# The copies of N to the substitution's tile: the order in which ScalarE walks them (RWKV-7 attention and a gated MLP, one core)

## The chip, the cores and the metric

The kernel runs on one core of one Trainium2 chip. The metric is the device time of one execution in microseconds (us); lower is better. The times are medians over several runs.

## The reference, cut to what matters

The first block is a recurrent attention (4 batches, 8 heads, 768 steps, head dimension 40). Each step reads from a 40x40 state per head and then updates it:

```python
y[:, :, t] = einsum('bhd,bhde->bhe', rt, state)
Sa = einsum('bhde,bhe->bhd', state, at)
state = state * wt[:, :, None, :] - einsum('bhd,bhe->bhde', Sa, bt) \
        + einsum('bhd,bhe->bhde', vt, kt)
```

Its output, as 3072 tokens of 320 numbers, goes through `h = x @ w_in` (320x2048), `g = h * cos(h)` and `g @ w_out` (2048x320). All of it is in float32; the two weights arrive in double precision and are rounded in the kernel.

## The kernel before, in words

The 768 steps are cut into chunks of 64 (C), and a "unit" u is one chunk of two batches with all eight heads, so there are 24 units. Within a chunk the step-by-step update becomes a triangular system: a matrix N of products of b and a between the steps of the chunk has to be inverted. The kernel inverts blocks of 32 (Q = 32) by a back substitution on VectorE, four units at a time, and joins the two blocks of a chunk with small matmuls (the tiles called `beside`).

N is made in `p1_n(u)`, for two units at a time. TensorE fills a PSUM tile `nps` whose word order is unit (written c), head (j) and step (t), with t innermost; the two halves of the heads (e) stand in two PSUM banks. From there ScalarE (called ACT in the profile) makes two kinds of copies:

- The diagonal blocks go to the SBUF tile `nt`, whose word order within a partition is step t, unit, e, j. Along t its step is 32 words. For the units 0 to 3 (L447) there are two copies of 128 partitions by 256 words for each call; for all later units (L455) there are four of 32 partitions by 512 words. With 24 units that is 4 copies of the first form and ten groups of four of the second.
- `lower()` (the segment `lo` of the plan, L466 and L474) later copies the other blocks to `noff` and `rt`. Both sides of these copies are walked in runs of 32 words or more.

Once four units stand in `nt`, `inv_start` (L493) turns it with one transpose of VectorE into `u`, and `inverse` runs 31 steps of two VectorE instructions (L501, L505), two transposes at the end (L518, L509) among them. The result is read by `beside_first` and `beside_second`, and by `ch_s`.

The order of work is written out by hand. A string, `PLAN`, lists segments (`pn4`, `lo4`, `k2`, `T1`, `M` for a piece of the MLP, `r` for one step of its cosine, `i` for a step of the inverse), and each engine takes its instructions in that order, with no reordering at run time. The PSUM tiles called `at` (`nps` except for unit 2, and the transposes, `gram`, `x0ps`, `sps`, `dps`, `qps`) share a pool of two buffers, so a later one of them waits until the copies out of the one before the last have been made. In the MLP, `ph` is the first product, `turns` its cosine argument (ACT L853, L860 and L861, VectorE L857), `gT` the product (VectorE L864) and `po` the second matmul.

The function that the diff touches, and what calls it:

Of the kernel before, what the change touches and what calls it, by code (L numbers as in the profile page):

```python
# [20 lines left out]
def kernel(  # L21
# [15 lines left out]
    Q = C // 2  # L37
    HB = Q // 2
    NB = P // C
    HH = H // 2  # L40
# [7 lines left out]
    quad = [slice(Q * i, Q * i + Q) for i in range(4)]  # L48
# [25 lines left out]
    def mm(o, lhsT, rhs, start, stop=True):  # L74
        nc.tensor.matmul(o, lhsT=lhsT, rhs=rhs, start=start, stop=stop, skip_group_check=True)  # L75

    def pick(t, offset, *dims):

        return bass.AP(t.tensor, t.offset + offset, [list(t.ap[0]), *(list(d) for d in dims)])
# [6 lines left out]
    G = {"rest": [], "outs": []}  # L86
# [15 lines left out]
    for n, fill in (("w", 1.0), ("a", 0.0), ("b", 0.0)):  # L102
        for i in range(4):
            x = slice((i - 2) * H * DP, (i - 1) * H * DP)
            if i < 2:
                t = const.tile([P, H, DP], F32, tag=f"nat_{n}{i}", name=f"nat_{n}{i}")
            else:
                t = {
                    "w": w_in_sb[:, 0, late:], "a": w_in_sb[:, 1, late:], "b": late_out
                }[n][:, x].rearrange("p (h d) -> p h d", h=H)  # L110
# [211 lines left out]
    def at(name):  # L322
        return ps_a.tile([P, 2, 512], F32, tag="at", name=name)

    def one(pool, name):
        if pool is None:
            return at(name)[:, 0]
        return pool.tile([P, 512], F32, tag="h" if pool is ps_h else "o", name=name)
# [81 lines left out]
    def p1_n(u):  # L410
        if u == 2:
            ps = [one(ps_h, "nps") for _ in range(2)]
        else:
            pair = at("nps")
            ps = [pair[:, e] for e in range(2)]


        for i in range(2):
            for j in range(4):
                o = (4 * i + j) * Q  # L420
                for bb in range(NB):
                    for e in range(2):
                        bT, aT = G["bT", u + i][half[e], j], G["aT", u + i][half[e], j]
                        if u >= 4:
                            mm(
                                pick(ps[e][blk[bb ^ e]], o, (8 * Q, 2), (1, Q)), bT[:, blk[bb]],
                                aT[:, blk[bb]], i == 0 and j == 0,
                            )
                            continue
                        for m in range(2):  # L430
                            x = slice(C * bb + Q * m, C * bb + Q * m + Q)
                            to = ps[e][quad[2 * (bb ^ e) + m]]
                            first = i == 0 and j == 0
                            if m:
                                mm(to[:, o : o + Q], bT[:, x], aT[:, x], first)
                            else:
                                mm(
                                    pick(to, o, (8 * Q, 2), (1, Q)), bT[:, x], aT[:, blk[bb]],
                                    first,
                                )  # L440

        if u % 4 == 0:
            G["nt"] = sb1.tile([P, Q, 4, 2, HH], F32, tag="nt", name="nt")
            G["rtq", u // 4] = sb2.tile([P, 4, H, C], F32, tag="rt", name="rt")
        if u < 4:
            for e in range(2):
                nc.scalar.copy(  # L447
                    G["nt"][:, :, u % 4 : u % 4 + 2, e, :].rearrange("p t c j -> p c j t"),
                    ps[e][:, : 2 * HH * Q].rearrange("p (c j t) -> p c j t", c=2, j=HH),
                )  # L450
        else:

            for n in range(4):
                o = 8 * Q * (n % 2)
                nc.scalar.copy(  # L455
                    G["nt"][quad[n], :, u % 4 : u % 4 + 2].rearrange("p t c e j -> p e c j t"),
                    pair[quad[n], :, o : o + 8 * Q].rearrange("p e (c j t) -> p e c j t", c=2, j=HH),
                )

        def lower():  # L460
            if u < 4:
                noff = late_out[:, Q * H * u : Q * H * (u + 2)].rearrange(
                    "p (c e j t) -> p c e j t", c=2, e=2, j=HH
                )
                for e in range(2):
                    nc.scalar.copy(  # L466
                        noff[:, :, e].rearrange("p c j t -> p c (j t)"),
                        ps[e][:, : 2 * HH * Q].rearrange("p (c n) -> p c n", c=2),
                    )
                G["noff", u // 2] = noff  # L470
            rt = G["rtq", u // 4]
            for g in range(NB):
                for e in range(2):
                    nc.scalar.copy(  # L474
                        rt[quad[2 * g], u % 4 : u % 4 + 2, HH * e : HH * e + HH, Q:],
                        ps[e][quad[2 * g], 8 * Q :].rearrange("p (c j t) -> p c j t", c=2, j=HH),
                    )

        G["lower", u] = lower
# [476 lines left out]
    def n_of(u):  # L956
        needs(f"pb{u}")
        p1_n(u)
# [254 lines left out]
```

## Time and profile before

| | |
|---|---|
| Median of 3 runs | 806.73 us (804.41 to 807.42) |
| The profiled execution's own time | 803.6 us |
| Its span, first to last instruction | 801.9 us |
| TensorE (PE) busy | 721.6 us, 90% of the span |
| VectorE (DVE) busy | 509.3 us, 64% |
| ScalarE (ACT) busy | 432.2 us, 54% |
| GpSimd (POOL) busy | 192.8 us, 24% |

The profiled execution is 3.1 us shorter than the median and 0.8 us shorter than the fastest of the three runs; it is one execution, and its durations are those of that one. In the first 165 us of the span PE is busy for 112 us and VectorE for 129 us; from 165 us on PE is busy for 610 of 637 us. ("x4" behind a group is the number of its instructions; "idle before" is the time in which the engine stood still just ahead of them, with what ended that.)

### The profile page before, as it was taken

How to read it: one execution, taken by the hardware profiler on the slowest of the kernel's cores; microseconds unless marked ns; L12 is line 12 of the kernel's file. 1: busy time of each engine (PE TensorE's matmuls, PEld its weight loads, DVE VectorE, ACT ScalarE, POOL GpSimd, SP SyncE). 2: the span in 40 equal slices, each digit the busy share in tenths (PEclk: the TensorE clock that was granted, in tenths of full speed). 3: DMA queues.
4: the chain of work that ended last, by engine and by line, in shares of the span. 5: the costliest groups of instructions: out<-in, count | busy, mean ns of one | idle time of the engine just before them, and what ended most of it. 6: DMA issues, size and time to landing. Idle time of an engine off the chain costs nothing.

```text
span 801.9 us, 27337 instructions
## 1 busy us (share of the span) xinstructions
PE 721.6 (90%) x11880; PEld 569.9 (71%) x11880; DVE 509.3 (64%) x969; ACT 432.2 (54%) x760; POOL 192.8 (24%) x305
## 2 busy tenths in 40 slices
PE   4538778979998998999999989999999999999995
PEld 3437666756776787778778768877878777877773
DVE  6896877799668885577873387854456673433331
ACT  0334468745586357674557555466574556353442
POOL 4233634340522243111232111232010320301000
PEclk9556799999999999999999999999999999999999
DMA  9534556442424334433421312330231111100000
GB/s 160 124 87 115 171 108 159 106 101 59 81 59 117 60 63 81 92 70 65 72 66 44 61 28 63 65 72 11 44 62 26 40 42 36 36 20 28 19 17 17
DMA packets 180536, 55.05 MB, mean 69 GB/s; under 512 B 154432, under 2 KB 176000, under 8 KB 180416
## 3 DMA queue, kind: packets, MB, share of 16 engines
q1 hardware_dynamic: 163328, 50.35, 28.4%
q10 hardware_dynamic: 16896, 2.62, 2.1%
q8 instruction: 94, 1.54, 0.8%
q0 software_dynamic: 192, 0.33, 0.3%
q14 instruction: 26, 0.21, 0.1%
HBM read 42.07 MB, written 11.14 MB: 66 GB/s over the span
## 4 chain that ended last, share of the span: by engine, by line
PE 67%; DVE 12%; ACT 10%; DMA 3%; issue 3%; SPq 2%; POOL 1%; ACTq 0%; DVEq 0%; POOLq 0%
PE po L75 22%; PE ph L75 22%; ACT nt L455 4%; PE x0ps L75 4%; PE dps L75 3%; PE gram L75 3%; PE beside L75 3%; PE vT L333 2%; PE sps L75 2%; DVE inv_tmp L501 2%; DVE inv L505 1%; PE qps L75 1%; PE nps L75 1%; DMA nat_a<-in_a_dram 1%; PE wT L333 1%
## 5 line engine op out<-in xcount | busy, mean ns | idle before, releaser
L75 PE MATMUL po<-w_out_sb,gT 128*128 128x320 f32 x768 | 225.0, 443 | 0.0
L75 PE MATMUL ph<-xT,w_in_sb 128*128 128x256 f32 x768 | 184.4, 389 | 3.6 <-DVE gT L864 3.5
L75 PEld LDWEIGHTS po<-w_out_sb,gT 128*128 128x128 f32 x768 | 142.7, 193 | 56.3 <-issue 4.6
L75 PEld LDWEIGHTS ph<-xT,w_in_sb 128*128 128x128 f32 x768 | 142.6, 192 | 30.6 <-issue 6.2
L853 ACT ACTIVATE turns<-ph,rnd 128x512 f32<-128x512 f32 x96 | 62.1, 685 | 134.0 <-PE ph L75 126.1
L857 DVE SCALAR_TENSOR_TENSOR turns<-turns,ph 128x512 f32<-128x512 f32 x96 | 63.8, 682 | 92.9 <-ACT turns L853 92.8
L864 DVE TENSOR_TENSOR gT<-ph,turns 128x512 f32<-128x512 f32 x96 | 65.3, 685 | 37.1 <-ACT turns L861 36.9
L773 POOL TENSOR_TENSOR qz<-qz,wc 128x160 f32<-128x160 f32 x44 | 21.2, 485 | 245.6 <-DVE qz L772 244.2
L861 ACT ACTIVATE turns<-turns,half_pi 128x512 f32<-128x512 f32 x96 | 69.3, 722 | 3.1
L860 ACT ACTIVATE turns<-turns 128x512 f32<-128x512 f32 x96 | 60.2, 628 | 16.7 <-DVE turns L857 13.0
L505 DVE TENSOR_TENSOR inv<-inv,inv_tmp 128x31 f32<-128x31 f32 (+15 forms) x155 | 61.4, 396 | 5.3
L501 DVE TENSOR_TENSOR inv_tmp<-u,inv 128x31 f32<-128x31 f32 (+15 forms) x155 | 60.3, 389 | 3.0
L75 PE MATMUL ph<-xT,w_in_tail 64*64 64x256 f32 (+1 forms) x704 | 52.4, 386 | 0.0
L455 ACT COPY nt<-nps 32x512 f32<-32x512 f32 x40 | 41.9, 1047 | 6.8 <-PE nps L75 6.4
L370 DVE RECIPROCAL rw<-nat_w 128x320 f32<-128x320 f32 x20 | 42.8, 2142 | 0.2 <-POOL kn L624 0.2
L788 POOL TENSOR_TENSOR yt<-yt,wb 128x512 f32<-128x512 f32 x24 | 31.4, 1310 | 38.4 <-DVE yt L783 38.4
L746 DVE TENSOR_TENSOR sm<-sps,su 128x256 f32<-128x256 f32 x48 | 18.1, 418 | 32.1 <-ACT sm L741 31.1
L75 PEld LDWEIGHTS ph<-xT,w_in_tail 64*64 64x64 f32 (+1 forms) x704 | 26.8, 138 | 15.9 <-issue 10.6
L724 DVE COPY x<-x0ps 128x416 f32<-128x416 f32 x24 | 14.1, 588 | 34.9 <-ACT x L723 34.9
L692 ACT COPY qz<-qps 40x512 f32<-40x512 f32 x44 | 25.4, 577 | 19.7 <-PE qps L75 19.3
L371 POOL TENSOR_TENSOR bn<-nat_b,rw 128x320 f32<-128x320 f32 x22 | 19.8, 901 | 65.3 <-DVE rw L370 38.0
L75 PEld LDWEIGHTS x0ps<-vvm,ag 64*64 64x64 f32 x768 | 19.6, 140 | 12.1 <-issue 7.9
(147 smaller groups left out, 1107.0 us busy)
## 6 DMA issues: line engine op xcount, KB each, us to landing
rp<-in_r_dram SPq DMA_DIRECT2D x96, 40.0 KB
vp<-in_v_dram SPq DMA_DIRECT2D x96, 40.0 KB
xd<-yt SPq DMA_DIRECT2D x48, 80.0 KB
out_dram<-ot SPq DMA_DIRECT2D x24, 160.0 KB
nat_k<-in_k_dram SPq DMA_DIRECT2D x42, 80.0 KB
ws<-in_w_dram SPq DMA_DIRECT2D x5, 640.0 KB
wd<-ws SPq DMA_DIRECT2D x5, 640.0 KB
xT<-xd SPq DMA_DIRECT2D x24, 128.0 KB
```

The source lines that it names most:

```text
L75: nc.tensor.matmul(o, lhsT=lhsT, rhs=rhs, start=start, stop=stop, skip_group_check=True)
L370: nc.vector.reciprocal(rw, wn)
L455: nc.scalar.copy(G["nt"][quad[n], :, u % 4 : u % 4 + 2].rearrange("p t c e j -> p e c j t"), pair[quad[n], :, o : o + 8 * Q].rearrange("p ...
L501: nc.vector.tensor_tensor(tmp, u[:, j : j + 1, :j].to_broadcast([P, Q - j, j]), x[:, j:, j : j + 1].to_broadcast([P, Q - j, j]), ALU.mult,)
L505: nc.vector.tensor_tensor(x[:, j:, :j], x[:, j:, :j], tmp, ALU.subtract)
L692: nc.scalar.copy(pick(z[rows], 0, (NZ - C, 2), (NZ, 2 * NB), (1, C)), ps[rows, :, : 2 * NB * C].rearrange("p f (i t) -> p f i t", t=C),)
L788: nc.gpsimd.tensor_tensor(yt.rearrange("p j b t -> p (j b) t"), yt.rearrange("p j b t -> p (j b) t"), wx, ALU.mult)
L853: nc.scalar.activation(n, u, ACTF.Identity, bias=rnd, scale=1.0)
L857: nc.vector.scalar_tensor_tensor(ns[e], ns[e], -ROUND, us[e], ALU.add, ALU.subtract)
L860: nc.scalar.activation(n, n, ACTF.Abs)
L861: nc.scalar.activation(n, n, ACTF.Sin, bias=half_pi, scale=-2.0 * math.pi)
L864: nc.vector.tensor_tensor(gT[:, 2 * e : 2 * e + 2].rearrange("p f t -> p (f t)"), us[e], ns[e], ALU.mult)
```

## The change

Both sides of each copy to `nt` are walked in another order. Before, the source is walked as it lies in PSUM (t innermost, runs of 32 neighbouring words), and the destination has a step of 32 words from one word to the next. After, the destination is walked as it lies in SBUF: runs of 4 words in the first form and of 16 words in the second, while the source has a step of 32 words from one word to the next, over j and c in one bank in the first form, and over j, e (the other bank) and c in the second. The words copied, the numbers of instructions, partitions and words in each, the engine and the plan stay as they are.

```diff
         if u < 4:
             for e in range(2):
                 nc.scalar.copy(
-                    G["nt"][:, :, u % 4 : u % 4 + 2, e, :].rearrange("p t c j -> p c j t"),
-                    ps[e][:, : 2 * HH * Q].rearrange("p (c j t) -> p c j t", c=2, j=HH),
+                    G["nt"][:, :, u % 4 : u % 4 + 2, e, :],
+                    ps[e][:, : 2 * HH * Q].rearrange("p (c j t) -> p t c j", c=2, j=HH),
                 )
         else:
 
             for n in range(4):
                 o = 8 * Q * (n % 2)
                 nc.scalar.copy(
-                    G["nt"][quad[n], :, u % 4 : u % 4 + 2].rearrange("p t c e j -> p e c j t"),
-                    pair[quad[n], :, o : o + 8 * Q].rearrange("p e (c j t) -> p e c j t", c=2, j=HH),
+                    G["nt"][quad[n], :, u % 4 : u % 4 + 2],
+                    pair[quad[n], :, o : o + 8 * Q].rearrange("p e (c j t) -> p t c e j", c=2, j=HH),
                 )
```

## The prediction

> **What bounds the kernel now.** I read the busy times first, then the chain of work that ended last. Both are on the page:
>
> ```profile
> PE 721.6 (90%) x11880; PEld 569.9 (71%) x11880; DVE 509.3 (64%) x969; ACT 432.2 (54%) x760; POOL 192.8 (24%) x305
> ...
> PE 67%; DVE 12%; ACT 10%; DMA 3%; issue 3%; SPq 2%; POOL 1%; ACTq 0%; DVEq 0%; POOLq 0%
> ```
>
> TensorE (PE) is the bound over the whole, and its 80 us of idle time are all that any other engine can give back. ScalarE (ACT) carries 10% of the chain, and the line of the chain by lines puts 4% of the span (32 us) on L455, one of the two lines changed; its 40 copies are busy for 41.9 us. So three quarters of that work lies on the chain. Next, the groups by shape on ACT. The columns are busy us and mean ns of one, then the idle time ahead:
>
> ```profile
> L455 ACT COPY nt<-nps 32x512 f32<-32x512 f32 x40 | 41.9, 1047 | 6.8 <-PE nps L75 6.4
> L474 ACT COPY rt<-nps 32x256 f32<-32x256 f32 x48 | 15.1, 360 | 0.2
> L645 ACT COPY kT<-kT 128x512 f32<-128x512 f32 x24 | 14.0, 585 | 6.0 <-PE kT L333 4.8 <-issue 1.1
> L618 ACT COPY rt<-beside 32x512 f32<-32x512 f32 x24 | 13.8, 575 | 2.5 <-PE beside L75 2.0
> L447 ACT COPY nt<-nps 128x256 f32<-128x256 f32 x4 | 2.1, 622 | 1.6 <-PE nps L75 1.6
> L466 ACT COPY w_out_sb<-nps 128x256 f32<-128x256 f32 x4 | 1.3, 376 | 1.1 <-DMA rp<-in_r_dram 1.1
> L348 ACT COPY w<-wT 128x8 f32<-128x8 f32 x4 | 0.5, 174 | 10.8 <-PE wT L333 10.8
> ```
>
> The first and fourth rows have the same engine, operation, shape and kind of tiles; only the order of the words written differs. Writing SBUF in steps of 32 words costs 1047 - 575 = 472 ns in 512 words, 0.92 ns a word. L447 against L466, both out of `nps`, says the same: 622 - 376 = 246 ns in 256 words, 0.96 ns a word. Whatever the other side costs, this is what the change takes away.
>
> **The instructions.** The copies stay 4 of 128x256 and 40 of 32x512, in the same places of ACT's order, and nothing moves on the other four engines; no wait is added. All that changes is the duration of one copy, and with it when its readers and the later work of ACT start.
>
> **The new duration.** No large copy in this trace reads PSUM in steps, so I bound it. Below: no row shows a stepped read beating a dense one, so 575 ns (L618) for the second form and 376 ns (L466) for the first are the lower end. Above: the only stepped read of PSUM on ACT is L348, 8 words 64 words apart, in 174 ns. A line through the 128-row copies (585 ns at 512 words, 376 at 256) gives 0.816 ns a word and 167 ns at none, so 174 ns at 8 words: no surcharge. A line through the 32-row copies (575 at 512, 360 at 256) gives 0.84 and 145; against that one, L348's 8 words take 29 ns, 3.6 ns each, and 512 would take 145 + 1850 = about 2000 ns. So the bounds are 575 and 2000 ns, and the copy gets slower than today's 1047 from about 1.75 ns a word. I take 575 to 620 ns, since L348 has 128 rows as the first line has. It is a weak witness: it also writes SBUF in steps, and 8 x 0.92 = 7 ns of that ought to show and doesn't, so eight words may just fit a buffer.
>
> VectorE's transposes of 128x1024 add a hint on steps in SBUF:
>
> ```profile
> L509 DVE STREAM_TRANSPOSE rt<-inv 128x1024 f32<-128x1024 f32 x6 | 11.7, 1944 | 0.0
> L518 DVE STREAM_TRANSPOSE rn<-inv 128x1024 f32<-128x1024 f32 x5 | 10.6, 2114 | 0.1
> L493 DVE STREAM_TRANSPOSE u<-nt 128x1024 f32<-128x1024 f32 x6 | 7.4, 1242 | 9.5 <-ACT nt L455 7.7 <-ACT nt L447 1.8
> ```
>
> L493 is dense on both sides, L509 writes in steps (+702 ns), L518 reads in steps as well (+170 more). There the step on the write is the dear one and that on the read the cheap one. But it is another engine and SBUF, and a read could hide under the slow write.
>
> The rule that speaks against the change is in the Trainium skill, page "PSUM — Partial Sum Buffer", section "Specifications (TRN2)": PSUM has lines of 8 bytes; the page "SBUF — State Buffer", section "Door 1: The DMA port swizzle", gives SBUF lines of 16 bytes, and says that full rate needs two accesses to a line. A step of 128 bytes has one access to a line in either memory, so by it the read would pay as the write did. The trace agrees for the write (1047 against 575 ns); for the read it has only L348. The rule comes back as the second rival.
>
> **What the path gets.** A group of four copies would end 4 x 472 = 1.89 us earlier. What that is worth is what stands still behind it, so I went through the timeline around each of the ten groups. Two of them, with the idle time of an engine and what ended it in brackets:
>
> ```profile
> 226.34 4.25 ACT L455 COPY nt<-nps 32x512 f32<-32x512 f32 x4
> ...
> 230.60 1.27 ACT L474 COPY rt<-nps 32x256 f32<-32x256 f32 x4
> ...
> 231.92 1.09 PE L333 MATMUL aps<-ident,nat_a 128*128 128x128 f32 x8 [1.14 <-ACT rt L474]
> ...
> 242.48 1.25 DVE L493 STREAM_TRANSPOSE u<-nt 128x1024 f32<-128x1024 f32 x1 [1.90 <-ACT nt L455]
> ...
> 250.01 0.94 PE L75 MATMUL x0ps<-vvm,ag 64*64 64x104 f32 x32 [1.79 <-DVE vvm L663]
> ```
>
> In the first, PE wants the buffer that `nps` holds, and gets it when the last `rt` copy has read it; PE has 1.14 us to win, then it is its own bound. In the second VectorE waits 1.90 us for `nt` and is then busy without a pause up to `vvm`, for which PE waits 1.79 us. Read so, group by group (start of the copies in us; what is won):
>
> - 128.8: `gram` waits 0.43 us for `kT`, which is behind the copies on ACT; VectorE then waits 2.39 us for a `sign` of the weights behind them, and PE 1.96 us for VectorE's `vvm`. 1.7.
> - 154.3: VectorE waits 3.22 and 0.97 us for ACT's `sign` and `turns`, and is on the chain from 161 to 184 us. The tails of `ph` end at 158.9 and hold `turns` there. 1.5.
> - 226.3: 1.14. 238.2: 1.8 (both shown).
> - 312.3: `kT` waits 1.47 us for `rt`. 1.47.
> - 342.9: `x0ps` waits 0.41 us for `s`, `qps` 0.22 us for `rt`. 0.63.
> - 426.3: PE does not stand still. 0.
> - 457.8: `kT` waits 2.15 us for VectorE's `sm`, which waits for ACT's `sm` right behind the copies. 1.85.
> - 544.7: `gram` waits 1.09 us for `kT`. 1.09.
> - 582.5: `qps` waits 1.74 us for `rt`. 1.74.
>
> That is 12.9 us. The two copies of the first form at 33.6 us have VectorE waiting 1.79 us for them; 2 x 246 ns is 0.5. Sum 13.4 us. I take 12: in the first two groups ACT, VectorE and the DMAs take turns on the chain, and one of them may be late for a reason of its own. So the profiled execution's 803.6 us would become 791.6, and since the median of the runs is 3.1 us above it, the median would become 794.7 us, 1.5% less. If everything that ACT saves arrived (ten times 1.89 and 1.0) it would be 19.9 us; if only PE's direct waits for ACT counted (0.43, 0.86 for `sT` at 162.95, 1.14, 0.42 for `vT` at 243.11, 1.47, 0.63, 1.09 and 1.74), 7.8.
>
> **Rivals.**
>
> First, slower: the stepped read costs more than the stepped write did. The place is the same ten groups, the price the duration of one copy, and it decides from 1.75 ns a word. ACT is the last to arrive behind nine of ten groups, so every microsecond more is paid in full there. Half way between 1.75 and the bound of 3.6 ns a word a copy takes 145 + 512 x 2.7 = 1530 ns, 480 ns more; nine groups of four make 17 us and the first form adds about one: 825 us. At the bound it is 36 us or so, 843. For it: the read order takes four words in one bank, then four in the other, a walk that no row of the trace has, and L348 has 8 words only. Against it: L348 on the line with the same row count, and the cheap read of L518.
>
> Second, no change: the read in steps runs at about half rate as the write did, 167 + 512 x 2 x 0.816 = 1003 ns, 44 ns less a copy, 0.18 us a group, at most 1.7 us in all: 805.5 us. This is what the skill's rule would make of it; for it speaks that the write shows just such a doubling.
>
> Third, the copies get faster but only the direct waits shrink, because VectorE's and the DMAs' own chains are as late as before: the 7.8 us above, 799 us. This is inside the forecast's side.
>
> **How the numbers follow.** Faster 0.62 (forecast 0.50 around 794.7, third rival 0.12); no change 0.12; slower 0.26. About 0.5%, 4 us, is what a measurement of this kernel can tell from no change. The forecast with the third rival spans 787 (all that ACT saves) to 800 or so. To leave out no more than 2 in 10 the range also takes in the case of no change, and the nearer part of the slower case, up to 818: a copy of about 1380 ns. The likeliest case alone is 787 to 800.
>
> **What would show it.** The rows of L455 and L447 in the profile after decide at once: 575 to 620 and 376 to 400 ns for the forecast, about 1000 for the second rival, above 1047 for the first. If they fall, ACT's busy time drops by some 20 us to 412, L455 leaves the chain, and the brackets above (`aps` behind `rt`, `u` behind `nt`, `qps` behind `rt`) shrink to nothing or name another engine. The forecast is wrong if L455 stays above 900 ns, or if it falls and those idle times of PE stay.

## The result, and the profile after

The changed kernel takes 792.3 us (median; 791.64 to 793.06), and the kernel before, run beside it, 805.57 us. The ratio is 0.9834, with a 95% interval of 0.9808 to 0.9861: 13.3 us less, where the forecast had 12. A second comparison, shown below, gave 0.9829 (0.9797 to 0.9861). The profiled execution took 791.87 us, with a span of 790.1. Two executions of the experiments below, of 944.9 and 1814.66 us where the others of their kernels took about 800, are left out of their ratios.

The busy times and the chain by engine, from the page after:

```profile
PE 715.3 (91%) x11880; PEld 566.6 (72%) x11880; DVE 512.3 (65%) x969; ACT 413.0 (52%) x760; POOL 193.7 (25%) x305
...
PE 72%; DVE 13%; ACT 5%; DMA 3%; issue 3%; SPq 1%; POOL 0%; ACTq 0%; DVEq 0%; POOLq 0%
```

ScalarE is busy for 19.2 us less, and its part of the chain is halved; L455 is gone from the chain by lines. The groups by shape on ACT (busy us and mean ns of one) say why:

```profile
L455 ACT COPY nt<-nps 32x512 f32<-32x512 f32 x40 | 23.0, 575 | 6.4 <-PE nps L75 6.0
...
L618 ACT COPY rt<-beside 32x512 f32<-32x512 f32 x24 | 13.8, 574 | 2.7 <-PE beside L75 2.4
L466 ACT COPY w_out_sb<-nps 128x256 f32<-128x256 f32 x4 | 1.3, 376 | 0.9 <-DMA rp<-in_r_dram 0.9
L447 ACT COPY nt<-nps 128x256 f32<-128x256 f32 x4 | 1.3, 370 | 1.1 <-PE nps L75 1.1
```

L455 fell from 1047 to 575 ns, the duration of the dense copy of the same shape (L618), and L447 from 622 to 370 ns, about that of L466 (376). The stepped read of PSUM costs nothing that these rows show.

The timeline after, at the two places that the prediction showed:

```profile
224.87 2.34 ACT L455 COPY nt<-nps 32x512 f32<-32x512 f32 x4
227.23 1.27 ACT L474 COPY rt<-nps 32x256 f32<-32x256 f32 x4
...
229.15 1.04 PE L333 MATMUL aps<-ident,nat_a 128*128 128x128 f32 x8
...
237.25 1.24 DVE L493 STREAM_TRANSPOSE u<-nt 128x1024 f32<-128x1024 f32 x1
237.33 2.91 POOL L173 TENSOR_TENSOR ws<-ws,we 128x1280 f32<-128x1280 f32 x1 [8.01 <-DVE ws L168]
...
238.53 1.76 DVE L501 TENSOR_TENSOR inv_tmp<-u,inv 128x31 f32<-128x31 f32 x1
...
246.46 1.21 PE L75 MATMUL x0ps<-vvm,ag 64*64 64x104 f32 x32 [2.38 <-DVE vvm L663]
```

At the first place the bracket behind `aps` (1.14 us before) is gone. At the second, the wait of VectorE for `nt` (1.90 us) is gone too, but PE's wait for `vvm` did not shrink: it grew from 1.79 to 2.38 us. VectorE starts 1.9 us earlier against PE's own work there, and now meets GpSimd's join of `ws` (L173), which had run beside VectorE's wait and its transpose before. The first step of the inverse takes 1.76 us instead of 0.69, and the second (L505, at 240.32 us) 0.80 instead of 0.36. Counted from the start of the copies, `vvm` is ready only 0.2 us earlier than before (11.43 us against 11.63), while PE arrives 0.8 us earlier (9.20 against 9.99), because its short waits for ScalarE ahead of that are gone (0.42 us for `kT` among them); so its wait grows.

What follows that wait is a second surprise. The stretches behind two waits, the one at 463 us in the kernel before and the one at 246 us in the kernel after (length, then busy us and number of instructions of PE, its weight loads, VectorE, ScalarE and GpSimd, then the granted clock, the DMA share and GB/s):

```profile
464.10:467.50 3.40, 3.40 (x8) 2.11 (x7) 2.77 (x8) 3.18 (x6) 0.00 (x0) 0.50 0.00 0
467.50:470.00 2.50, 2.50 (x11) 1.74 (x10) 1.81 (x6) 0.72 (x1) 0.00 (x0) 1.00 0.00 0
```

```profile
247.10:250.50 3.40, 3.40 (x51) 2.65 (x44) 3.23 (x8) 2.40 (x4) 0.00 (x0) 0.51 0.81 230
250.50:252.00 1.50, 1.50 (x16) 0.82 (x19) 0.90 (x3) 0.14 (x1) 0.00 (x0) 1.00 0.40 69
```

After a stop of PE of 2.15 and of 2.38 us the granted clock is halved for 3.4 us. As an estimate, a PE that is busy all that time loses half of it, about 1.7 us; the experiments below measure 1.4 to 1.8. So a wait's price was not only its own length. In these two executions the kernel before paid this at 463 us, and the kernel after no longer does; it pays at 246 us instead.

### The profile page after: what moved, and what is told of

The parts are those of the page before. It is cut to its first block, busy times and chain, and to the rows that moved or that the text cites. A ratio compares the mean times of both kernels' runs of the same rounds, so it can differ in the third digit from the quotient of the medians.

```text
span 790.1 us, 27337 instructions
## 1 busy us (share of the span) xinstructions
PE 715.3 (91%) x11880; PEld 566.6 (72%) x11880; DVE 512.3 (65%) x969; ACT 413.0 (52%) x760; POOL 193.7 (25%) x305
## 4 chain that ended last, share of the span: by engine, by line
PE 72%; DVE 13%; ACT 5%; DMA 3%; issue 3%; SPq 1%; POOL 0%; ACTq 0%; DVEq 0%; POOLq 0%
PE ph L75 25%; PE po L75 24%; PE dps L75 4%; PE x0ps L75 4%; PE gram L75 2%; PE vT L333 2%; PE beside L75 2%; DVE inv_tmp L501 2%; PE sps L75 2%; DMA nat_a<-in_a_dram 2%; DVE inv L505 1%; DVE rw L370 1%; PE qps L75 1%; PE nps L75 1%; PE aps L333 1%
## 5 line engine op out<-in xcount | busy, mean ns | idle before, releaser
L75 PE MATMUL po<-w_out_sb,gT 128*128 128x320 f32 x768 | 222.6, 439 | 0.0
L75 PE MATMUL ph<-xT,w_in_sb 128*128 128x256 f32 x768 | 185.1, 390 | 3.8 <-DVE gT L864 3.7
L75 PEld LDWEIGHTS po<-w_out_sb,gT 128*128 128x128 f32 x768 | 141.3, 191 | 55.4 <-issue 3.0
L75 PEld LDWEIGHTS ph<-xT,w_in_sb 128*128 128x128 f32 x768 | 143.1, 193 | 31.2 <-issue 6.2
L505 DVE TENSOR_TENSOR inv<-inv,inv_tmp 128x31 f32<-128x31 f32 (+15 forms) x155 | 61.3, 395 | 5.3
L501 DVE TENSOR_TENSOR inv_tmp<-u,inv 128x31 f32<-128x31 f32 (+15 forms) x155 | 62.5, 403 | 3.0
L75 PE MATMUL ph<-xT,w_in_tail 64*64 64x256 f32 (+1 forms) x704 | 52.2, 386 | 0.0
L75 PEld LDWEIGHTS ph<-xT,w_in_tail 64*64 64x64 f32 (+1 forms) x704 | 26.5, 137 | 16.0 <-issue 10.3
L724 DVE COPY x<-x0ps 128x416 f32<-128x416 f32 x24 | 14.1, 588 | 33.6 <-ACT x L723 33.6
L75 PE MATMUL dps<-vvm,kn 64*64 64x104 f32 x768 | 23.6, 263 | 4.6 <-DVE sm L746 4.1
L75 PEld LDWEIGHTS x0ps<-vvm,ag 64*64 64x64 f32 x768 | 18.6, 134 | 12.0 <-issue 8.5
```

Source lines behind the costliest of these rows:

```text
L501: nc.vector.tensor_tensor(tmp, u[:, j : j + 1, :j].to_broadcast([P, Q - j, j]), x[:, j:, j : j + 1].to_broadcast([P, Q - j, j]), ALU.mult,)
L505: nc.vector.tensor_tensor(x[:, j:, :j], x[:, j:, :j], tmp, ALU.subtract)
```

## The experiments

**Which groups pay.** Three kernels give the new order to a part of the units only, each by a condition such as this one:

```diff
+                if u in (4, 6):
+                    nc.scalar.copy(  # the new order
+                        ...
+                    )
+                    continue
                 nc.scalar.copy(  # the order of before
```

> Only the copies of the units 4 and 6 (the two earliest groups of four) take the new order; all else is as before. Theory (a group ends 1.89 us earlier, and what stands still behind it moves up): 3.2 us less than before by the prediction's 1.7 and 1.5. Rival (only the direct waits of the tensor engine for the scalar engine shrink, 0.43 and 0.86): 1.3 us less. Rival (paid in full): 3.8 us less. The copies of these groups measure 575 ns, the others 1047 ns.

> Only the copies of the units 8, 10, 12 and 14 take the new order (226, 238, 312 and 343 us in the trace of before). Theory as the prediction has it: 1.14 + 1.8 + 1.47 + 0.63 = 5.0 us less. Theory as the trace of after corrects it: the vector engine, started 1.9 us earlier at 238 us, runs into GpSimd's join of ws, the tensor engine waits 2.4 us for vvm and its granted clock then falls to 0.50, so the second group brings nothing or costs up to 1.5: about 1.14 + 0 + 1.47 + 0.63 = 3.2 us less, or 1.7. Rival (direct waits only): 3.7 us less. The granted clock right behind 248 us tells the first two apart.

> Only the copies of the units 16, 18, 20 and 22 take the new order (426, 458, 545 and 583 us before). Theory as predicted: 0 + 1.85 + 1.09 + 1.74 = 4.7 us less. Theory as the trace of after corrects it: the wait of 2.15 us at 461 us is also what lets the granted clock fall to 0.63 and 0.81 behind it before, so removing it brings some 1.7 us more: 6.4 us less. Rival (direct waits only): 2.8 us less. The granted clock from 463 to 470 us tells the first two apart: 1.00 if the correction holds.

Measured against before: the units 4 and 6 give 0.9965 (0.9942 to 0.9987), that is 2.8 us, between 1.0 and 4.7; the units 8 to 14 give 0.9973 (0.9948 to 0.9998), 2.2 us (0.2 to 4.2); the units 16 to 22 give 0.9939 (0.9914 to 0.9964), 4.9 us (2.9 to 6.9). The first and the last hold the predicted 3.2 and 4.7 us. The first also holds both its rivals (1.3 and 3.8 us); the last also holds the 6.4 us with the clock, and leaves the 2.8 us of the direct waits just outside. The middle one excludes the predicted 5.0 us, and holds the corrected 1.7 to 3.2 us and the 3.7 us of the direct waits.

The traces tell more, since a stretch can be measured from the start of one group of copies to the next. From the group at 426 us to the end, the old order took 373.8 us in each of the first two of these kernels, where the wait of 2.15 us at `kT` is there but the clock does not fall behind it, and 375.6 us in the kernel before, where it does. With the new order it takes 368.8 us in the third and 369.1 in the kernel after. So the predicted waits give 4.9 us (4.7 predicted), and the fall of the clock 1.8 us on top where it happens. From the group at 226 us to the one at 426 us the old order took 199.9, 199.4 and 199.2 us, and the new order 196.2 (after) and 196.1 (second kernel), both with the clock at half behind `vvm`: 3.4 us less, not the 5.0 of the prediction. Taken apart from group to group, those at 226, 312 and 343 us brought 1.9, 1.7 and 1.1 us, more than the 1.14, 1.47 and 0.63 listed. From the group at 238 us to the next the old order took 73.4 to 74.1 us, and the new one 75.1 and 75.2 with the clock's fall, and 73.8 in a later run of it without (the last experiment): this group brought nothing, and the fall cost about 1.4 us. The clock behind `kT` in the third kernel is 1.00 from 467 to 472 us. It is at full rate, as expected, but so it is in the two kernels with the wait. So a fall does not follow every such wait; the last experiment comes back to this.

From the first group (129 us) to the third (226 us) the old order took 97.6, 96.8 and 98.6 us, and the new order 92.2 (after) and 92.6 (first kernel). That is 5 us, more than the listed 3.2. In all three traces of the old order the clock falls at the wait for `vvm` that follows the first group, in the two of the new order it does not. Two later kernels with the new order (the five steps ahead of `g7`, and the new order again) settle what is the clock's: theirs falls twice in this stretch, as that of the kernel before does, at partly other places, and they take 94.2 and 94.6 us. That is 3.0 to 3.3 us less than the kernel before, which is the listed 3.2.

**The same copies, made twice.**

```diff
-            for n in range(4):
+            for n in (0, 0, 1, 1, 2, 2, 3, 3):
```

> The new order, but each of the 40 copies of 32x512 is made twice, one right after the other, which gives the scalar engine back the time that the new order saved: 2 x 575 = 1150 ns a pair against 1047 ns of one copy before. Theory (the gain is the scalar engine's time and nothing else): near before, about 3 us over it: 10 groups x 4 x 0.1 us less the 0.5 us of the first form, 808 to 810 us. Rival (what the slow writes cost others, by holding the SBUF or the tile, is the gain): stays near after, 792 to 796 us.

Measured: 813.48 us, ratio 1.0113 (1.0081 to 1.0145). So the gain is ScalarE's time, and the rival is out: with the new order but the time given back, nothing of the 13 us is left. That it is 9 us slower than before, and not 3, has to be explained. Eight copies take 4.78 us, 0.54 us more than the four of before, which is 5 us in nine groups. The waits behind them are longer by as much (`kT` 2.77 us, `gram` 1.68, `qps` 2.24), and the clock falls behind three of the later ones. Behind 130 us, and without the last few us, it is at half for 24 us in this trace, against 10 in that of the kernel before. Behind the group at 317 us, for instance:

```profile
322.00:326.00 4.00, 2.63 (x116) 2.56 (x120) 0.69 (x1) 3.93 (x9) 0.90 (x2) 0.82 0.59 157
326.00:330.00 4.00, 4.00 (x31) 2.70 (x24) 3.35 (x4) 0.97 (x2) 0.00 (x0) 0.50 0.17 68
```

**The steps alone.** A kernel that holds nothing but copies, four of each, with TensorE idle:

> No part of the computation: single copies of 512 words on 128 partitions, four of each, first on the scalar engine and then on the vector engine, with one side walked in steps (read PSUM by 2, 4, 32 words; write SBUF by 2, 4, 8, 32; both by 32; read SBUF by 4, 32; write PSUM by 32), copies of 8 words dense and in steps of 64 on either side, and the two forms of the 32x512 copy with the tensor engine idle; the output is not the reference's. Theory (a step on the write to SBUF is what costs, a step on the read of PSUM costs nothing): scalar engine 585 ns dense and for every PSUM step, about 1050 for an SBUF write step of 32 with or without a stepped read; 575 and 1047 ns for the kernel's two forms. Rival (any step costs, and the kernel's new form escapes because it takes turns between two banks): about 1000 ns for the PSUM step of 32 in one bank. Eight words: if the stepped write shows 7 ns more than the dense one, the 8-word row could have shown a price; if not, it could not.

The rows of ScalarE for 512 words on 128 partitions. L60 is dense on both sides; L63 reads PSUM in steps of 32 words; L64 and L65 write SBUF in steps of 2 and 4; L68 does both in steps of 32, and L73 writes PSUM so. L96 and L97 are the new and the old form of the kernel's copy, and L74, L75 and L76 copy 8 words, dense, with a stepped read and with a stepped write:

```profile
L65 ACT COPY sout<-pair 128x512 f32<-128x512 f32 x4 | 4.2, 1055 | 0.1
...
L68 ACT COPY sout<-pair 128x512 f32<-128x512 f32 x4 | 4.1, 1015 | 0.1
L97 ACT COPY sout<-pair 32x512 f32<-32x512 f32 x4 | 4.0, 1005 | 0.1
...
L64 ACT COPY sout<-pair 128x512 f32<-128x512 f32 x4 | 2.4, 608 | 0.1
L73 ACT COPY pout<-sin 128x512 f32<-128x512 f32 x4 | 2.4, 589 | 0.1
...
L63 ACT COPY sout<-pair 128x512 f32<-128x512 f32 x4 | 2.3, 586 | 0.1
...
L60 ACT COPY sout<-pair 128x512 f32<-128x512 f32 x4 | 2.3, 586 | 3.3 <-DVE sout L45 3.2
L96 ACT COPY sout<-pair 32x512 f32<-32x512 f32 x4 | 2.3, 575 | 46.8 <-DVE sout L93 46.7
...
L76 ACT COPY sout<-pair 128x8 f32<-128x8 f32 x4 | 0.7, 173 | 0.1
L75 ACT COPY sout<-pair 128x8 f32<-128x8 f32 x4 | 0.7, 166 | 0.1
L74 ACT COPY sout<-pair 128x8 f32<-128x8 f32 x4 | 0.7, 164 | 0.1
```

In PSUM a step of any length measured is all but free, on the read (586 ns for 2, 4 and 32 words) and on the write (589 for 32). It is not the change of banks that saves the new form, for L63 stays in one bank. In SBUF a step of 2 words on the write costs 22 ns in 512 words. With steps of 4, 8 and 32 words on the write the copy takes 1015 to 1073 ns, and with steps of 4 and 32 on the read 1060 to 1088, against 617 for a dense read of SBUF; a stepped read of PSUM adds nothing to that (L68). VectorE shows the same pattern: 691 to 692 ns for reads of PSUM, dense and in all steps, 1054 for an SBUF write in steps of 4, and 1014 for one of 32. And 8 words do show the price of a stepped write: 173 against 164 ns. The kernel's old form takes 1005 ns here and 1047 in the kernel; the cause of that difference is open.

**Why the group at 238 us brought nothing.** Three kernels change the plan, on top of the new order.

```diff
-pn10 i i M i o k6 i i lo10 wj3 i i i M v7 g6 M i ag6 r r r q6 i M i i i r K7 ws3 xa6 k7 ...
+pn10 i i M i o k6 i i lo10 i i i M v7 g6 M i ag6 r r r q6 i M i i i r K7 wj3 ws3 xa6 k7 ...
```

> The new order, and in the plan GpSimd's join of ws (2.9 us, at 237 us) is moved behind the kn of unit 7, nothing else. Theory (a vector instruction with two SBUF operands stands still while GpSimd works, which is why the first steps of the inverse take 1.76 and 0.80 us there against 0.20 elsewhere): the first two steps take about 0.2 to 0.9 us, vvm is ready about 1.5 us earlier, and the wait of 2.4 us at 246 us falls to about 1; 789 to 792 us. The join then stretches whatever vector work stands beside it later. Rival (those steps are long for another reason, such as u just having been written): their durations stay at 1.7 and 0.8 us.

Measured: 792.62 us, 0.9839 (0.9813 to 0.9865), the same as the new order. From its timeline:

```profile
240.34 0.19 DVE L505 TENSOR_TENSOR inv<-inv,inv_tmp 128x31 f32<-128x31 f32 x1
...
242.43 2.93 POOL L173 TENSOR_TENSOR ws<-ws,we 128x1280 f32<-128x1280 f32 x1
242.62 2.86 DVE L505 TENSOR_TENSOR inv<-inv,inv_tmp 128x112 f32<-128x112 f32 x1
```

The first steps fell to 0.19 us each, so it was GpSimd that had stretched them: the join the first, and by the timeline after its next instruction, `kn` (0.88 us), the second. But the join now stands against a later step, which takes 2.86 us instead of 0.28 and ends 0.1 us behind it. `vvm` was no earlier (0.9 us later, counted from the copies), and PE's wait was 3.29 us, not the 1 us expected: the block moved with the join. The Trainium skill, page "SBUF — State Buffer", section "Terms", says that VectorE and GpSimd share a pair of SBUF ports, held by one for a whole instruction while the other stands still; by that rule the step has to wait out the join, and the trace agrees (2.86 against 2.93 us).

The next kernel takes five of the inverse's steps out of the way of `g6`, first to places ahead of `g7`:

```diff
-pn10 i i M i o k6 i i lo10 wj3 i i i M v7 g6 M i ag6 r r r q6 i M i i i r K7 ws3 xa6 k7 Lk8 wf4 r i Lv8 M i i Lr9 i t7
+pn10 i i M i o k6 lo10 wj3 M v7 g6 M i ag6 r r r q6 i M i i i r K7 ws3 xa6 k7 i i Lk8 wf4 r i Lv8 M i i i i Lr9 i i t7
```

> The new order, and in the plan five of the inverse's steps that stand between pn10 and g6 are moved behind g6 and q6, so that the vector engine reaches ag and vvm of unit 6 earlier. Theory (the gain of the group at 238 us was lost because vvm is late: the tensor engine stands still for 2.4 us at 246 us, and the granted clock may fall to 0.50 for one stretch of 3.4 us behind it): that wait falls under 1 us, the clock stays at 1.00 there, and the time falls by 1.5 to 4 us from the new order's, to 788 to 791 us. Rival (the steps are only late somewhere else, and the wait reappears behind the later turns): within 1 us of the new order.

Measured: 795.01 us, 0.9869 (0.9841 to 0.9898), no better than the new order (2.4 us over the kernel with the later join, which ran beside it). The wait at 246 us is gone, but the rival was right about the wait, if not about "within 1 us":

```profile
260.54 1.67 PE L75 MATMUL dps<-vvm,kn 64*64 64x104 f32 x32 [4.52 <-DVE vvm L663]
```

The moved steps stand ahead of the next unit's `vvm` now, and the clock is at half for 6.8 us at this wait. The last pair puts them behind `g7`, one by one, and runs the new order again beside it:

```diff
-pn10 i i M i o k6 i i lo10 wj3 i i i M v7 g6 ... T6 M i r K8 ag7 ... q7 r M i i M r X6 i i r
+pn10 i i M i o k6 lo10 wj3 M v7 g6 ... T6 i M i i r K8 ag7 ... q7 r i M i i i M r X6 i i i r
```

> The new order, and five steps of the inverse are moved from between pn10 and g6 to places behind g7. Theory (in the first attempt the moved steps stood ahead of g7 and made its vvm late by 4.5 us at 260 us): both waits for vvm, at 246 and at 260 us, are under 1 us, the granted clock stays at 1.00 from 240 to 300 us, and the time is 1.5 to 4 us under the new order's: 788 to 791 us. Rival (the vector engine is the bound in this stretch, so the steps are late wherever they are put): a wait of over 2 us for some vector result later on, and no less than 792 us.

> The new order itself, once more, for the comparison on this chip. 790 to 794 us as before. Theory (the granted clock halves for stretches of 3.4 us after some stops of the tensor engine of about 2 us, not after all): the same wait of about 2.4 us for vvm at 246 us, with or without a fall of the clock behind it.

Measured: 788.18 us, 0.9777 (0.9752 to 0.9802), against 792.89 us, 0.9829 (0.9797 to 0.9861), for the new order again. The two intervals overlap only at their edges, so this version beats both kernels, by 4.7 us over the new order in the medians. The traces show 1.5 us of that, against this second trace of the new order, and 2.4 against the first, in the stretch with the moved steps (193.8 us from the third group to the seventh, against 195.2 and 196.2); where the rest comes from is not shown. Neither `x0ps` at 242.6 us nor `dps` at 254.2 has a wait in its trace, and the clock holds (busy time by engine, then the clock, as above):

```profile
243.00:248.00 5.00, 5.00 (x102) 3.79 (x95) 3.07 (x9) 4.27 (x9) 0.00 (x0) 1.00 0.67 173
248.00:258.00 10.00, 9.90 (x194) 8.19 (x193) 9.16 (x23) 3.53 (x9) 0.54 (x2) 1.00 0.22 36
```

In the new order's second trace the wait for `vvm` is 2.36 us at 251.8 us, all but the 2.38 of the first; behind it the clock stays up:

```profile
252.50:255.90 3.40, 3.40 (x69) 2.40 (x64) 3.23 (x8) 2.69 (x5) 0.00 (x0) 1.00 0.87 240
```

The ten traces of the whole kernel show what tells the two apart. In each of them every change of the granted clock lies on a grid of its own, with steps of 3.41 us. Here is the step of that grid that holds the wait in the trace after, and the two over which the same wait is spread in the second trace of the new order:

```profile
243.59:247.00 3.41, 1.03 (x27) 0.66 (x29) 3.24 (x10) 0.69 (x1) 0.00 (x0) 1.00 0.49 83
```

```profile
246.82:250.23 3.41, 2.64 (x24) 1.64 (x16) 3.03 (x12) 1.37 (x2) 0.01 (x1) 1.00 0.82 247
250.23:253.64 3.41, 1.81 (x66) 1.68 (x67) 3.38 (x8) 0.64 (x2) 0.00 (x0) 1.00 0.32 68
```

PE is busy for 0.30 of the step in the first, and for 0.77 and 0.53 in the second. Over all ten traces, except their last few us, the clock fell after each of the 22 steps at full clock in which PE was busy for less than 0.44 of the time, after 42 of the 85 between 0.44 and 0.63, and after none of the 1905 above. By these counts a stop of about 2 us costs more when it falls into one step than when a border cuts it; between 0.44 and 0.63 PE's busy time alone does not decide.

## Why the prediction was right, and where it was not

- **The price of the write.** Right: the copies gave back 472 and 252 ns of the forecast 472 and 246.
- **The price of the read.** The lower bound (575 ns) was the truth, and the rivals that hang on this price, slower and no change, are out. The hint from L509 and L518 was no evidence for it. On VectorE a stepped read of SBUF is indeed the cheaper one (596 ns against 427 dense, where a stepped write takes 1014 against 692), but on ScalarE it costs as much as a stepped write (1060 against 617 dense), and neither says anything of PSUM. The reasoning about L348 was wrong in one point: eight words do pay for a stepped write. The row of 174 ns is the dense 164 with the 9 ns of its stepped write, and a stepped read alone adds 2 ns. The row was a good witness, but only the dense 8-word copy shows that, and the trace of before had none. The line through the 128-row copies had put 174 ns where a dense copy takes 164.
- **The rule of the Trainium skill that the prediction cites.** Read as a rule for the copies, it would have made them take about 1003 ns. The 16 bytes of a line of SBUF agree with the runs (a step of 2 words nearly free, one of 4 not); the 8 bytes of PSUM show in no copy of ScalarE or VectorE that was measured.
- **The sum over the groups.** 13.4 us by the list, 12 taken, 13.3 measured: in part this was luck, since terms were wrong and made up for each other. The group at 238 us was put at 1.8 us and brought nothing; PE's wait for `vvm` grew instead, because VectorE, early, ran into GpSimd's work. That step read the trace of before as if VectorE's next instructions kept their durations. The groups at 226, 312 and 343 us brought 4.7 us, where the list has 3.2. Added up over the stretches, with the clock's falls kept out, the ten groups come to about 12.7 us (an estimate), against 12.9 listed. And no term held the granted clock. In the profiled pair the kernel before pays three falls of 3.4 us behind 130 us (at 140, 184 and 464 us) and the kernel after one (at 247 us), which by the estimate of 1.7 us each is about 3.4 us in the kernel after's favour. What the falls add to the medians is not known, since they differ from one execution to the next.
- **The list from 426 us on** was right within 0.2 us where the clock takes no part (4.9 us measured, 4.7 listed). `kT` waits 0.34 us instead of 2.15, and the waits of `gram` and `qps` are gone.
- **The third rival** (only the direct waits, 7.8 us) is out by the whole, 13.3 us (11.2 to 15.5), and by the group at 458 us, which brought its 1.8 us though PE there waits for VectorE and not for ScalarE.
- **What stays open.** In the first 130 us the traces differ by more than this change can: inside `gram` at 60 us PE stops with nothing that it waits for named in the profile, for 0.9 to 1.3 us in four of the traces (before among them) and for 3.0 to 4.2 us in six others (after among them). So the profiled pair's own gain of 11.8 us holds about 2.9 us of this against the change. Its cause was not tried. For the same reason no run shows the 0.5 us of the first form's two copies at 33.6 us.

## What to carry to other kernels

When a copy of float32 from PSUM to SBUF on ScalarE or VectorE has to change the order of words, put the step on the PSUM side; here that nearly halved ScalarE's copy, and one row tells whether it is needed: that of a dense copy of the same shape. Sum up what stands still behind a faster instruction, group by group, rather than its busy time, but also ask what each earlier engine runs into, since a stall can only move. And a stop of TensorE of about 2 us cost nearly twice its length here where it fell into one step of the clock's grid, and where it falls differed between two executions of the same kernel.

## What the runs showed of the hardware that was not expected

- Steps in PSUM are free for reads by ScalarE and VectorE: 586 and 691 to 692 ns for 512 words, dense or in steps of 2, 4 or 32. Steps of 4 to 32 words in SBUF take ScalarE to 1015 to 1088 ns, on either side.
- A GpSimd `tensor_tensor` of 2.9 us holds back a VectorE `tensor_tensor` on SBUF for its whole length (2.86 us for a step of 0.28), but not the transpose of VectorE, which took 1.24 us beside it.
- The granted clock falls to 0.50 for 3.4 us, or a multiple of it, behind some stops of PE and not behind others as long (one of 2.77 us, with the copies made twice, had none): of the waits of 2.36 to 2.38 us for `vvm`, two of three had it, and of those of 2.14 to 2.15 us at `kT`, one of three. It also fell behind two stops of 1.4 us. The Trainium skill, page "TensorE: Matmul & The Clock Gate", section "Part 1: The HAM clock gate (the "warmup" mystery)", tells of a free-running window of about 3.4 us in which activity is watched; by that rule the fall would hang on where the stop lies in the window. The traces agree, with the grid of 3.41 us and the 22, 85 and 1905 steps counted above. No run shifted a stop along the grid and left all else as it was.
